# Who transposes x's second contraction tile: TensorE or the DMA, and which queue loads what first

## The chip, the cores and the metric

One core of a Trainium2 chip runs the whole kernel. The metric is the device time of one execution in microseconds. Five engines take part: TensorE (PE; its weight loads are shown as PEld), VectorE (DVE), ScalarE (ACT), GpSimd (POOL) and SyncE (SP). SP and ACT each issue DMAs on a queue of their own.

## What is computed

```python
x:  (1, 2048, 640) bf16;  w1: (640, 1728) bf16;  w2: (1728, 640) bf16
h = jnp.einsum("bsd,df->bsf", x, w1)
h = jax.nn.silu(h)
out = jnp.einsum("bsf,fd->bsd", h, w2)
```

## The kernel before

The program is a list of operations (`add(engine, emit, deps, group)`), written out by hand. Each engine executes its own operations in the order in which they were added, and before each it waits for the semaphores of its `deps`. A DMA's `group` names its semaphore. Nothing reorders the work.

TensorE needs x with the contraction on the partitions, so x is transposed into `xT_sb` in tiles of 128 contraction rows by 512 rows of x (`SCH`). There are five contraction tiles (`DT`, counted 0 to 4) and four chunks of 512 rows (`NSC`, counted from 0). Two ways of transposing are in use:

- by TensorE: x's tile is loaded as it is into `x0_sb`, four 128x128 transposes (L182) against `ident` put it into a bank of PSUM, and DVE (L186) or ACT (L188) copies it to `xT_sb`. Chunk 0 does this for tiles 0 and 1. Tile 0 is loaded in two halves, `x0_a` on SP and `x0_b` on ACT, and is copied in two halves; tile 1 is `x0_c`, on ACT.
- by DMA: `transpose_x` (L152) issues a transposing DMA on SP that reads x in HBM and writes `xT_sb`. Chunk 0 does this for tiles 2, 3 and 4 (`x0_2` to `x0_4`), the other chunks for all five.

w1 is loaded on SP: the first 6 column tiles (`FA`) of each contraction tile by itself (`w1_0` to `w1_4`, 192 KB each), the rest in `w1_a` (column tiles 6 and 7) and `w1_b` (8 to 13). On SP the order is x0_a, w1_0, w1_1, w1_2, x0_2, w1_3, x0_3, w1_4, x0_4, w1_a, w1_b, and then the transposes of chunk 1, the first of which waits for w1_a.

On TensorE come warm-up matmuls on constants (L172), the transposes of tile 0, two more warm-up matmuls, and then `column_group` (L263): for each contraction tile in turn six matmuls of 128x512, one into each of six banks. The first matmul of each contraction tile waits for x's tile and w1's tile. After the second matmul of a contraction tile, `between` is called, and there `transpose_next` puts the four transposes of the next tile, if TensorE transposes it: this is the case for tile 1 alone. `unit` (L221) does the other column tiles, five matmuls each, the first of which waits for w1_a or w1_b. ACT (sigmoid, L205) and DVE (multiplication, L208) make `hT_sb` from the banks. Chunk 1 begins with a second `column_group`, and chunks 2 and 3 use `unit` throughout. Last comes the product with w2 (L326), copied out (L337, L339) and stored (L299).

Of the kernel before, what the change touches and what calls it, by code (L numbers as in the profile page):

```python
# [20 lines left out]
class Plan:  # L21
# [9 lines left out]
    def add(self, eng, emit, deps=(), group=None):  # L31
        op = Op(eng, emit, [d for d in deps if d is not None], group)
        self.ops.append(op)
        return op
# [40 lines left out]
def bass_standalone__dense_activation_silu__prompt_kernel(  # L75
# [6 lines left out]
    bf16 = mybir.dt.bfloat16  # L82
    fp32 = mybir.dt.float32

    xf = x.flatten_outer_dims()
    of = out.flatten_outer_dims()
    S, D = xf.shape
    F = w1.shape[1]
    P = 128
    H = P // 2  # L90
    SCH = 512
    DT = D // P
# [5 lines left out]
    JB = SCH // P  # L98
# [4 lines left out]
    with ExitStack() as es:  # L103
        def sb(name, shape, dtype):
            return es.enter_context(nc.sbuf_tensor(name, shape, dtype))

        xT_sb = sb("xT_sb", [P, DT, S], bf16)
# [3 lines left out]
        NSIG = 4  # L111
        sig_sb = sb("sig_sb", [P, NSIG, SCH], bf16)
        o_sb = sb("o_sb", [P, ST, D], bf16)
        x0_sb = sb("x0_sb", [P, JB, D], bf16)
        ident = sb("ident", [P, P], bf16)
        warm_sb = sb("warm_sb", [P, 32], fp32)
        oT_sb = sb("oT_sb", [P, NSC, SCH], bf16)
        ps = es.enter_context(nc.psum_tensor("ps", [P, NBANK, SCH], fp32))

        w1_v = w1.rearrange("(dt p) f -> p dt f", p=P)  # L120
        x0_v = xf[0:SCH, :].rearrange("(j p) d -> p j d", p=P)
        w2_v = w2[0:FR * P, :].rearrange("(ft p) d -> p ft d", p=P)

        plan = Plan()
        add = plan.add
        bank_free = [[] for _ in range(NBANK)]
        turn = [0]

        def take_bank():
            b = turn[0] % NBANK  # L130
            turn[0] += 1
            return b


        FA = 6
        w1_cuts = [FA, 8, FT]
        id_a = add("pool", lambda e: e.memset(ident[:, :], 0.0))
        id_b = add("pool", lambda e: e.affine_select(
            out=ident[:, :], in_=ident[:, :], compare_op=ALU.not_equal, fill=1.0,
            base=0, pattern=[[-1, P]], channel_multiplier=1), [id_a])  # L140
        warm = add("dve", lambda e: e.memset(warm_sb[:, :], 0.0))

        def load_x0(eng, name, j0, j1, d0, d1):
            return add(eng, lambda e: e.dma_start(
                out=x0_sb[:, j0:j1, d0 * P:d1 * P], in_=x0_v[:, j0:j1, d0 * P:d1 * P]), group=name)

        def load_w1(eng, name, d0, d1, f0, f1, deps=()):
            return add(eng, lambda e: e.dma_start(
                out=w1_sb[:, d0:d1, f0:f1], in_=w1_v[:, d0:d1, f0:f1]), deps, group=name)

        def transpose_x(sc, dt, name, deps=()):
            return add("sp", lambda e: e.dma_start_transpose(  # L152
                out=xT_sb[:, dt, sc * SCH:(sc + 1) * SCH],
                in_=xf[sc * SCH:(sc + 1) * SCH, dt * P:(dt + 1) * P]), deps, group=name)

        x0_a = [load_x0("sp", "x0_a", 0, JB // 2, 0, 1), load_x0("act", "x0_b", JB // 2, JB, 0, 1)]
        w1_lo = [load_w1("sp", "w1_0", 0, 1, 0, FA * P)]
        x0_c = load_x0("act", "x0_c", 0, JB, 1, 2)
        w1_lo += [load_w1("sp", f"w1_{dt}", dt, dt + 1, 0, FA * P) for dt in (1, 2)]
        add("act", lambda e: e.activation(out=warm_sb[:, :], in_=warm_sb[:, :], func=ACT.Sigmoid), [warm])  # L160
        x0_t = {2: transpose_x(0, 2, "x0_2")}
        for dt in (3, 4):
            w1_lo.append(load_w1("sp", f"w1_{dt}", dt, dt + 1, 0, FA * P))
            x0_t[dt] = transpose_x(0, dt, f"x0_{dt}")
# [5 lines left out]
        def warm_up(columns):  # L170
            for n in columns:
                add("pe", lambda e, n=n: e.matmul(  # L172
                    ps[:, NBANK - 1, 0:n], lhsT=ones[:, 0:P], rhs=ones[:, 0:n], start=True, stop=True))

        warm_up([SCH] * 5 + [2 * P])

        def transpose_x0(dt, j0, j1, b):

            dst = ps[:, b, :].bitcast(bf16)[:, j0 * P:j1 * P]
            out = xT_sb[:, dt, j0 * P:j1 * P]  # L180
            for j in range(j0, j1):
                t = add("pe", lambda e, j=j: e.transpose(  # L182
                    dst[:, (j - j0) * P:(j - j0 + 1) * P], x0_sb[:, j, dt * P:(dt + 1) * P], ident[:, :]),
                    [x0_a[j // (JB // 2)], id_b] if dt == 0 else [x0_c] + bank_free[b])
            if dt % 2 == 0:
                c = add("dve", lambda e: e.tensor_copy(out=out, in_=dst), [t])  # L186
            else:
                c = add("act", lambda e: e.copy(out=out, in_=dst), [t])  # L188
            bank_free[b] = [c]
            return c  # L190

# [10 lines left out]
        def silu(b, parts, n, pe):  # L202
            s = sig_turn[0] % NSIG
            sig_turn[0] += 1
            a = add("act", lambda e: e.activation(  # L205
                out=sig_sb[:, s, 0:n], in_=ps[:, b, 0:n], func=ACT.Sigmoid), [pe, sig_free[s]])
            for rows, ft, cols in parts:
                v = add("dve", lambda e, rows=rows, ft=ft, cols=cols: e.tensor_tensor(  # L208
                    out=hT_sb[rows, ft, cols], in0=ps[rows, b, 0:n], in1=sig_sb[rows, s, 0:n],
                    op=ALU.mult), [a])  # L210
                chunk_done[cols.start // SCH] = v
                if ft == FR:
                    tail_done[cols.start // SCH] = v
            bank_free[b] = [v]
            sig_free[s] = v
# [25 lines left out]
        for sc in range(1, NSC):  # L241
# [4 lines left out]
            if sc == 2:  # L246
                half = FR // 2
                for a, z in ((0, half), (half, FR)):
                    w2_dma.append(add("sp", lambda e, a=a, z=z: e.dma_start(
                        out=w2_sb[:, a:z, :], in_=w2_v[:, a:z, :]), group="w2"))  # L250
                for hh in range(2):
                    w2_dma.append(add("sp", lambda e, hh=hh: e.dma_start(
                        out=w2_sb[hh * H:(hh + 1) * H, FR, :], in_=w2[FR * P:F, :]), group="w2"))

        def column_group(sc, x_dep, w1_dep, between=None):

            banks = [take_bank() for _ in range(FA)]
            for dt in range(DT):
                for ft in range(FA):
                    deps = bank_free[banks[ft]] if dt == 0 else []  # L260
                    if ft == 0:
                        deps = deps + [x_dep[dt], w1_dep[dt]]
                    pe = add("pe", lambda e, dt=dt, ft=ft: e.matmul(  # L263
                        ps[:, banks[ft], :], lhsT=w1_sb[:, dt, ft * P:(ft + 1) * P],
                        rhs=xT_sb[:, dt, sc * SCH:(sc + 1) * SCH],
                        start=(dt == 0), stop=(dt == DT - 1)), deps)
                    if dt == DT - 1:
                        silu(banks[ft], [(slice(0, P), ft, slice(sc * SCH, (sc + 1) * SCH))], SCH, pe)
                    if between and ft == 1:
                        between(dt + 1)  # L270

        def transpose_next(dt):
            if dt in x0_t:
                x0T.append(x0_t[dt])
            elif dt < DT:
                x0T.append(transpose_x0(dt, 0, JB, FA + dt % 2))

        half = [transpose_x0(0, k * JB // 2, (k + 1) * JB // 2, FA - 2 + k) for k in range(2)]
        x0T = [half[1]]
        warm_up([SCH, 2 * P])  # L280
        column_group(0, x0T, w1_lo, transpose_next)
        for ft in range(FA, FR):
            unit(0, ft, 0, SCH)

        for sc in range(1, NSC):
            if sc == 1:
                column_group(sc, x1_of, w1_lo)
            for ft in range(FA if sc == 1 else 0, FR):
                unit(sc, ft, 0, SCH)
# [112 lines left out]
```

## Time and profile before

| What | Value |
|---|---|
| median of 3 runs | 125.84 us (125.55 to 126.11) |
| the profiled execution | 126.19 us, span 124.8 us |
| TensorE busy | 121.7 us (97%), 890 matmuls |
| DVE, ACT busy | 44.7 us (36%), 38.8 us (31%) |
| DMA | 10.41 MB, mean 83 GB/s over the span |
| transposing DMAs of x (L152) | 18, issue 1.12 to 2.60 us each, landing 2.7 to 7.1 us after the start of the issue |

The profile is one execution on the chip. Times in a timeline count from the start of the span. An entry with SPq or ACTq is the issue of a DMA; when its data are there is a separate figure, the landing, counted from the start of the issue. A matmul's time holds its way through the array, so successive matmuls overlap, and the pace of TensorE is read from their starts. The profiled time is 1.4 us longer than the span; that part lies around the span.

### The profile page before, as it was taken

What the parts mean: (1) busy time and instruction counts of PE and PEld (TensorE: products, weight loads), DVE (VectorE), ACT (ScalarE), POOL (GpSimd) and SP (SyncE); (2) the same over time, 40 slices, a digit from 0 to 9 for tenths busy, and PEclk for the clock granted to TensorE, in tenths of its full rate; (3) what the DMA queues carried; (4) which work ended last, traced back from release to release, by engine and by line L of the source; (5) the groups of instructions that cost most, each with busy time, mean ns of one, the idle gap of its engine ahead of it and who ended that gap; (6) DMA issues with size and microseconds to landing.
All of it is one profiled execution on the core that took longest, in us unless ns stands there. A gap on an engine that the chain in (4) does not pass through costs nothing.

```text
span 124.8 us, 2074 instructions
## 1 busy us (share of the span) xinstructions
PE 121.7 (97%) x890; PEld 57.1 (46%) x890; DVE 44.7 (36%) x70; ACT 38.8 (31%) x68; POOL 0.7 (1%) x6
## 2 busy tenths in 40 slices
PE   7999999999999999999999999999999999999992
PEld 2444444444444444444444444444444444446481
DVE  0102984079666666666682020202021020202021
ACT  4104953097555555555530010101011010101021
POOL 2000000000000000000000000000000000000000
PEclk9999999999999999999999999999999999999999
DMA  3989682559980000000000001115120201102434
GB/s 69 293 179 347 141 102 54 114 100 373 349 170 3 0 5 0 3 0 0 0 0 5 0 2 30 26 21 181 39 105 5 105 0 21 33 15 74 158 104 112
DMA packets 20201, 10.41 MB, mean 83 GB/s; under 512 B 14432, under 2 KB 20192, under 8 KB 20192
## 3 DMA queue, kind: packets, MB, share of 16 engines
q1 hardware_dynamic: 19104, 9.95, 30.0%
q10 hardware_dynamic: 1088, 0.33, 1.1%
q8 instruction: 7, 0.11, 0.4%
q14 instruction: 2, 0.02, 0.1%
HBM read 4.77 MB, written 2.62 MB: 59 GB/s over the span
## 4 chain that ended last, share of the span: by engine, by line
PE 98%; DVE 0%; issue 0%
PE ps L326 47%; PE ps L221 35%; PE ps L263 11%; PE ps L172 3%; PE ps L231 2%; PE ps L182 1%; DVE o_sb L337 0%
## 5 line engine op out<-in xcount | busy, mean ns | idle before, releaser
L326 PE MATMUL ps<-w_sb,hT_sb 64*128 64x512 bf16 (+2 forms) x486 | 47.3, 352 | 0.0
L208 DVE TENSOR_TENSOR hT_sb<-ps,sig_sb 128x512 bf16<-128x512 f32 (+1 forms) x56 | 37.0, 688 | 25.3 <-ACT sig_sb L205 25.3
L221 PE MATMUL ps<-xT_sb,w_sb 128*128 128x512 bf16 x200 | 43.5, 379 | 0.0
L205 ACT ACTIVATE sig_sb<-ps 128x512 bf16<-128x512 f32 x54 | 30.7, 606 | 27.5 <-PE ps L221 16.4
L326 PEld LDWEIGHTS ps<-w_sb,hT_sb 64*128 64x128 bf16 x486 | 23.5, 94 | 23.5
L221 PEld LDWEIGHTS ps<-xT_sb,w_sb 128*128 128x128 bf16 x200 | 19.6, 98 | 23.6
L337 DVE CAST o_sb<-ps 128x512 bf16<-128x512 f32 (+2 forms) x9 | 5.7, 632 | 37.6 <-PE ps L326 37.6
L339 ACT CAST o_sb<-ps 128x512 bf16<-128x512 f32 (+2 forms) x9 | 4.8, 538 | 38.6 <-PE ps L326 38.6
L263 PE MATMUL ps<-xT_sb,w_sb 128*128 128x512 bf16 x60 | 14.1, 392 | 0.0
L326 PE MATMUL ps<-hT_sb,w_sb 64*128 64x512 bf16 x108 | 12.3, 376 | 0.0
L263 PEld LDWEIGHTS ps<-xT_sb,w_sb 128*128 128x128 bf16 x60 | 5.9, 101 | 7.4 <-DVE xT_sb L186 0.7
L326 PEld LDWEIGHTS ps<-hT_sb,w_sb 64*128 64x128 bf16 x108 | 5.2, 94 | 6.5 <-issue 0.4
L337 DVE CAST oT_sb<-ps 128x512 bf16<-128x512 f32 x2 | 1.4, 692 | 11.7 <-PE ps L326 11.7
L339 ACT CAST oT_sb<-ps 128x512 bf16<-128x512 f32 x2 | 1.2, 585 | 13.6 <-PE ps L326 13.6
L172 PE MATMUL ps<-const-bfloat16-1.0 128*128 128x512 bf16 (+1 forms) x8 | 3.4, 575 | 0.8 <-PEq L387 0.8
L231 PE MATMUL ps<-xT_sb,w_sb 128*64 128x512 bf16 x20 | 2.3, 381 | 0.0
L172 PEld LDWEIGHTS ps<-const-bfloat16-1.0 128*128 128x128 bf16 x8 | 1.0, 140 | 1.8 <-issue 1.8
L160 ACT ACT_TABLE_LOAD x1 | 1.3, 1283 | 1.8 <-issue 1.8
L231 PEld LDWEIGHTS ps<-xT_sb,w_sb 128*64 128x64 bf16 x20 | 1.0, 110 | 1.2 <-issue 0.4
L186 DVE COPY xT_sb<-ps 128x256 bf16<-128x256 bf16 x2 | 0.5, 292 | 2.6 <-PE ps L182 2.6
L182 PEld LDWEIGHTS ps<-ident,x_sb 128*128 128x128 bf16 x8 | 1.0, 144 | 0.9 <-DMA x_sb<-in_x_dram 0.6
L188 ACT COPY xT_sb<-ps 128x512 bf16<-128x512 bf16 x1 | 0.6, 585 | 2.5 <-PE ps L182 2.5
(9 smaller groups left out, 2.5 us busy)
## 6 DMA issues: line engine op xcount, KB each, us to landing
out_dram<-o_sb SPq DMA_DIRECT2D x14, 160.0 KB, 1.9
w_sb<-in_w_dram SPq DMA_DIRECT2D x1, 1120.0 KB, 7.7
w_sb<-in_w_dram SPq DMA_DIRECT2D x5, 192.0 KB, 3.1
w_sb<-in_w_dram SPq DMA_DIRECT2D x1, 960.0 KB, 5.6
w_sb<-in_w_dram SPq DMA_DIRECT2D x1, 880.0 KB, 5.5
w_sb<-in_w_dram SPq DMA_DIRECT2D x1, 320.0 KB, 3.7
xT_sb<-in_x_dram SPq DMA_TRANSPOSE x18, 3.0
o_sb<-oT_sb SPq DMA_TRANSPOSE x16, 2.3
```

Of the source, the lines that this page charges most:

```text
L160: add("act", lambda e: e.activation(out=warm_sb[:, :], in_=warm_sb[:, :], func=ACT.Sigmoid), [warm])
L172: add("pe", lambda e, n=n: e.matmul(ps[:, NBANK - 1, 0:n], lhsT=ones[:, 0:P], rhs=ones[:, 0:n], start=True, stop=True))
L182: t = add("pe", lambda e, j=j: e.transpose(dst[:, (j - j0) * P:(j - j0 + 1) * P], x0_sb[:, j, dt * P:(dt + 1) * P], ident[:, :]), [x0_a[j ...
L188: c = add("act", lambda e: e.copy(out=out, in_=dst), [t])
L205: a = add("act", lambda e: e.activation(out=sig_sb[:, s, 0:n], in_=ps[:, b, 0:n], func=ACT.Sigmoid), [pe, sig_free[s]])
L208: v = add("dve", lambda e, rows=rows, ft=ft, cols=cols: e.tensor_tensor(out=hT_sb[rows, ft, cols], in0=ps[rows, b, 0:n], in1=sig_sb[rows, ...
L221: pe = add("pe", lambda e, dt=dt: e.matmul(ps[:, b, 0:n], lhsT=w1_sb[:, dt, ft * P:(ft + 1) * P], rhs=xT_sb[:, dt, cols], start=(dt == 0), ...
L231: pe = add("pe", lambda e, dt=dt, hh=hh: e.matmul(ps[hh * H:(hh + 1) * H, b, :], lhsT=w1_sb[:, dt, FR * P:F], rhs=xT_sb[:, dt, (sc + hh) * ...
L263: pe = add("pe", lambda e, dt=dt, ft=ft: e.matmul(ps[:, banks[ft], :], lhsT=w1_sb[:, dt, ft * P:(ft + 1) * P], rhs=xT_sb[:, dt, sc * SCH:( ...
L326: pe = add("pe", lambda e, b=b, n=n, lhsT=lhsT, rhs=rhs, ft=ft: e.matmul(ps[:, b, 0:n], lhsT=lhsT, rhs=rhs, start=(swap == 0 and ft == 0), ...
L337: ev = add("dve", lambda e, b=b, n=n, dst=dst: e.tensor_copy(out=dst, in_=ps[:, b, 0:n]), [pe])
L339: ev = add("act", lambda e, b=b, n=n, dst=dst: e.copy(out=dst, in_=ps[:, b, 0:n]), [pe])
```

## The change

Contraction tile 1 of chunk 0 is transposed by a DMA, `x0_1`, which becomes the first on SP's queue. x's tile 0 is loaded by one DMA of 128 KB instead of two halves, first on ACT's queue, and w1's tile 0 follows it there instead of on SP. The load x0_c, the four TensorE transposes of tile 1 and ACT's copy of them go, and `column_group` has no `between` any more. One of the two warm-up matmuls behind the transposes of tile 0, that of 256 columns, goes as well. `x0_sb` keeps one tile instead of five. In the changed kernel the lines after the loads have moved up: L172 becomes L168, L182 L178, L186 L180, L221 L213 and L263 L255.

```diff
--- before.py
+++ after.py
@@ -111,14 +111,14 @@
         NSIG = 4
         sig_sb = sb("sig_sb", [P, NSIG, SCH], bf16)
         o_sb = sb("o_sb", [P, ST, D], bf16)
-        x0_sb = sb("x0_sb", [P, JB, D], bf16)
+        x0_sb = sb("x0_sb", [P, JB, P], bf16)
         ident = sb("ident", [P, P], bf16)
         warm_sb = sb("warm_sb", [P, 32], fp32)
         oT_sb = sb("oT_sb", [P, NSC, SCH], bf16)
         ps = es.enter_context(nc.psum_tensor("ps", [P, NBANK, SCH], fp32))
 
         w1_v = w1.rearrange("(dt p) f -> p dt f", p=P)
-        x0_v = xf[0:SCH, :].rearrange("(j p) d -> p j d", p=P)
+        x0_v = xf[0:SCH, 0:P].rearrange("(j p) d -> p j d", p=P)
         w2_v = w2[0:FR * P, :].rearrange("(ft p) d -> p ft d", p=P)
 
         plan = Plan()
@@ -140,10 +140,6 @@
             base=0, pattern=[[-1, P]], channel_multiplier=1), [id_a])
         warm = add("dve", lambda e: e.memset(warm_sb[:, :], 0.0))
 
-        def load_x0(eng, name, j0, j1, d0, d1):
-            return add(eng, lambda e: e.dma_start(
-                out=x0_sb[:, j0:j1, d0 * P:d1 * P], in_=x0_v[:, j0:j1, d0 * P:d1 * P]), group=name)
-
         def load_w1(eng, name, d0, d1, f0, f1, deps=()):
             return add(eng, lambda e: e.dma_start(
                 out=w1_sb[:, d0:d1, f0:f1], in_=w1_v[:, d0:d1, f0:f1]), deps, group=name)
@@ -153,12 +149,12 @@
                 out=xT_sb[:, dt, sc * SCH:(sc + 1) * SCH],
                 in_=xf[sc * SCH:(sc + 1) * SCH, dt * P:(dt + 1) * P]), deps, group=name)
 
-        x0_a = [load_x0("sp", "x0_a", 0, JB // 2, 0, 1), load_x0("act", "x0_b", JB // 2, JB, 0, 1)]
-        w1_lo = [load_w1("sp", "w1_0", 0, 1, 0, FA * P)]
-        x0_c = load_x0("act", "x0_c", 0, JB, 1, 2)
+        x0_t = {1: transpose_x(0, 1, "x0_1")}
+        x0_a = add("act", lambda e: e.dma_start(out=x0_sb[:, :, :], in_=x0_v), group="x0_a")
+        w1_lo = [load_w1("act", "w1_0", 0, 1, 0, FA * P)]
         w1_lo += [load_w1("sp", f"w1_{dt}", dt, dt + 1, 0, FA * P) for dt in (1, 2)]
         add("act", lambda e: e.activation(out=warm_sb[:, :], in_=warm_sb[:, :], func=ACT.Sigmoid), [warm])
-        x0_t = {2: transpose_x(0, 2, "x0_2")}
+        x0_t[2] = transpose_x(0, 2, "x0_2")
         for dt in (3, 4):
             w1_lo.append(load_w1("sp", f"w1_{dt}", dt, dt + 1, 0, FA * P))
             x0_t[dt] = transpose_x(0, dt, f"x0_{dt}")
@@ -174,18 +170,14 @@
 
         warm_up([SCH] * 5 + [2 * P])
 
-        def transpose_x0(dt, j0, j1, b):
+        def transpose_x0(j0, j1, b):
 
             dst = ps[:, b, :].bitcast(bf16)[:, j0 * P:j1 * P]
-            out = xT_sb[:, dt, j0 * P:j1 * P]
+            out = xT_sb[:, 0, j0 * P:j1 * P]
             for j in range(j0, j1):
                 t = add("pe", lambda e, j=j: e.transpose(
-                    dst[:, (j - j0) * P:(j - j0 + 1) * P], x0_sb[:, j, dt * P:(dt + 1) * P], ident[:, :]),
-                    [x0_a[j // (JB // 2)], id_b] if dt == 0 else [x0_c] + bank_free[b])
-            if dt % 2 == 0:
-                c = add("dve", lambda e: e.tensor_copy(out=out, in_=dst), [t])
-            else:
-                c = add("act", lambda e: e.copy(out=out, in_=dst), [t])
+                    dst[:, (j - j0) * P:(j - j0 + 1) * P], x0_sb[:, j, :], ident[:, :]), [x0_a, id_b])
+            c = add("dve", lambda e: e.tensor_copy(out=out, in_=dst), [t])
             bank_free[b] = [c]
             return c
 
@@ -252,7 +244,7 @@
                     w2_dma.append(add("sp", lambda e, hh=hh: e.dma_start(
                         out=w2_sb[hh * H:(hh + 1) * H, FR, :], in_=w2[FR * P:F, :]), group="w2"))
 
-        def column_group(sc, x_dep, w1_dep, between=None):
+        def column_group(sc, x_dep, w1_dep):
 
             banks = [take_bank() for _ in range(FA)]
             for dt in range(DT):
@@ -266,19 +258,11 @@
                         start=(dt == 0), stop=(dt == DT - 1)), deps)
                     if dt == DT - 1:
                         silu(banks[ft], [(slice(0, P), ft, slice(sc * SCH, (sc + 1) * SCH))], SCH, pe)
-                    if between and ft == 1:
-                        between(dt + 1)
-
-        def transpose_next(dt):
-            if dt in x0_t:
-                x0T.append(x0_t[dt])
-            elif dt < DT:
-                x0T.append(transpose_x0(dt, 0, JB, FA + dt % 2))
-
-        half = [transpose_x0(0, k * JB // 2, (k + 1) * JB // 2, FA - 2 + k) for k in range(2)]
-        x0T = [half[1]]
-        warm_up([SCH, 2 * P])
-        column_group(0, x0T, w1_lo, transpose_next)
+
+        half = [transpose_x0(k * JB // 2, (k + 1) * JB // 2, FA - 2 + k) for k in range(2)]
+        x0T = [half[1]] + [x0_t[dt] for dt in range(1, DT)]
+        warm_up([SCH])
+        column_group(0, x0T, w1_lo)
         for ft in range(FA, FR):
             unit(0, ft, 0, SCH)
```

## The prediction

> **What bounds the kernel now.** I read the page's busy time and chain first, then the chain in order of time, then the timeline of the first 14 us and the landing of each DMA issued there. TensorE is busy 121.7 of 124.8 us and the chain is TensorE's all the way, so only two things can move the end: fewer cycles on TensorE, or a wait in front of it.
>
> From the page and the chain in order of time (start, us, what):
>
> ```profile
> PE 98%; DVE 0%; issue 0%
> PE ps L326 47%; PE ps L221 35%; PE ps L263 11%; PE ps L172 3%; PE ps L231 2%; PE ps L182 1%; DVE o_sb L337 0%
> ...
> 4.35 1.01 PE ps L263 x2
> 5.36 0.43 PE ps L182 x4
> 5.79 6.27 PE ps L263 x28
> 12.06 7.55 PE ps L221 x35
> 19.61 6.47 PE ps L263 x30
> ```
>
> The change ends before 12.06: from there the matmuls are the same in number and order. The first group of 30 (L263) takes 7.7 us from 4.35, the second, the same 30 matmuls, 6.47. The difference is the four transposes (L182, 0.43) and a slow start. The timeline (start, us, engine, line) shows the rest:
>
> ```profile
> 0.73 0.46 SPq L144 DMA_DIRECT2D x_sb<-in_x_dram  x1
> 0.74 1.03 ACTq L144 DMA_DIRECT2D x_sb<-in_x_dram  x2
> 0.77 2.51 PE L172 MATMUL ps<-const-bfloat16-1.0 128*128 128x512 bf16 x6 [0.77 <-PEq L387]
> 1.26 1.40 SPq L148 DMA_DIRECT2D w_sb<-in_w_dram  x3
> 2.70 1.21 SPq L152 DMA_TRANSPOSE xT_sb<-in_x_dram  x1
> 2.92 0.52 PEld L182 LDWEIGHTS ps<-ident,x_sb 128*128 128x128 bf16 x4 [0.33 <-DMA x_sb<-in_x_dram]
> 3.53 0.51 DVE L186 COPY xT_sb<-ps 128x256 bf16<-128x256 bf16 x2 [2.63 <-PE ps L182]
> ...
> 4.32 0.14 PEld L263 LDWEIGHTS ps<-xT_sb,w_sb 128*128 128x128 bf16 x2 [0.67 <-DVE xT_sb L186]
> 4.35 1.01 PE L263 MATMUL ps<-xT_sb,w_sb 128*128 128x512 bf16 x2
> ...
> 7.52 1.15 SPq L148 DMA_DIRECT2D w_sb<-in_w_dram  x2
> ```
>
> The six warm-up matmuls start 0.42 us apart. In narrow windows the L263 matmuls start at 4.35, 4.73, 5.58, 6.01, 6.28, and from 6.28 on eight take 1.89, 0.216 apart. So TensorE runs at half its later pace until about 6.1, 5.3 us after its first matmul, while the granted clock in the rows reads 1.00 throughout. DVE is done at 4.04, so the wait put down to it at 4.32 is really w1_0 (issue to landing, us):
>
> ```profile
> w_sb<-in_w_dram SPq DMA_DIRECT2D x1, 192.0 KB, 3.0
> x_sb<-in_x_dram ACTq DMA_DIRECT2D x1, 128.0 KB, 3.3
> xT_sb<-in_x_dram SPq DMA_TRANSPOSE x1, 3.7
> w_sb<-in_w_dram SPq DMA_DIRECT2D x1, 320.0 KB, 3.7
> w_sb<-in_w_dram SPq DMA_DIRECT2D x1, 880.0 KB, 5.5
> ```
>
> These are w1_0 (issued 1.26, landed 4.2), x0_c (1.27), the transpose x0_2 (2.70), and w1_a and w1_b. w1_a is issued at 7.52 and lands at 11.2, 0.7 before its matmul at 11.90. w1_b is issued at 8.15 and lands at 13.6; its matmul comes ten later, at 14.06, and that one's weights load one matmul ahead, at 13.84. So w1_b has about 0.2 us to spare, the least of the lead-in.
>
> **Part by part.**
>
> *Four TensorE transposes and the 256-column warm-up go.* The transposes take 0.43 us at half pace, between the second and third matmul. Matmuls move into that place and leave from the fast stretch: 0.43 of slow time is one matmul, worth 0.216 later. Gain 0.21 us. The warm-up (0.21) filled the wait for w1_0; without work ready it becomes idle time and costs nothing. ACT's copy L188 (0.58) goes too, off the path: its tile was ready at 6.41, for a matmul at 6.72.
>
> *x's tile 0 whole on ScalarE's queue.* Same 128 KB as the two halves, which landed after 2.1 and 2.3 us, but x0_1 moves another 128 KB beside it on the other queue. Below: 2.3 (landed 3.04). Above: 3.7, the transpose beside weight loads (4.4). In the stretch from 2.86 to 4.35 the DMA moved 296 GB/s, so 128 KB more is 0.44 us; I take 2.8, landing at 3.55, nearest to the half loads because nothing stands ahead of it on its queue. All four transposes now wait for all of it. The warm-up matmuls run out at 3.07: an idle hole of 0.5 us. From the first transpose to the last copy's end took 0.96 (3.07 to 4.04), so tile 0 is ready at 4.5; the warm-up matmul that is left covers most of that.
>
> *w1's tile 0 on ScalarE's queue.* Second there, issued again at 1.27 since the first issue takes 0.5. Ahead of it on its queue stand 128 KB instead of 64; on the other queue x0_1 replaces half of tile 0 and x0_c. Below: 2.95, as now (4.2). Above: 0.44 for a whole tile more (4.65). I take 4.6, since x0_1 now comes ahead of it where x0_c came beside it. First matmul 4.65 instead of 4.35.
>
> The sum for the group: starts 4.65, 5.08, 5.50, 5.93, fast from 6.2. Four matmuls are out by 6.2; before, four were out by 6.28. So 0.3 us of delay at half pace costs 0.15, the missing transposes return 0.21: the group ends 0.06 to 0.08 earlier.
>
> *x0_1 first on SyncE's queue.* A transpose takes 1.12 to 1.26 us to issue (2.70 to 3.95 with the gap behind it); it replaces x0_a and w1_0, which held SP from 0.73 to 1.75. Everything behind moves 0.2 later: w1_1, w1_2, x0_2, w1_3, x0_3, w1_4, x0_4, w1_a, w1_b and the x1 transposes. x0_1 itself lands 3.0 to 3.7 after issue, by 4.4; it is needed at 4.65 + 6 x 0.43 less the faster pace, about 6.5. w1_1 (5.1, then 5.3), x0_2 (6.4, then 6.6, for about 7.8) and w1_3 to x0_4 (9.3, then 9.5, for 10.5) all land over a microsecond early or nearly so. w1_a at 11.45 still leads its weight load at 11.6. **w1_b is what is late next**: 13.8 against a weight load wanted at 13.77. It takes back 0 to 0.1. x1_0 goes from 14.57 to 14.8, needed at 19.4. Nothing else moves past a queue; POOL and DVE keep their work.
>
> Total: 0.07 gained, 0.05 given back: no change, with ends of -0.35 (all lands as early as now, w1_b hidden) and +0.3. The profiled execution is 126.19 us with a span of 124.8; 1.4 lie around it. The three runs have a median of 125.84, 0.35 below it. On the median: 125.8.
>
> **Rivals.**
>
> *Early data (0.14).* Both loads land as now; the first matmul starts at 4.1. For it: the bytes up to w1_0 are nearly the same. Gain 0.21 + 0.12, of which w1_b, due then at 13.5, takes back up to 0.3: 125.5.
>
> *Late data (0.12).* x0_a and w1_0 are held up by the transpose on the other queue, by up to a microsecond (3.7 instead of 2.8). For it: x0_2, issued right behind w1_2, is the slowest 128 KB of the lead-in. The hold costs half while TensorE is slow: 0.5 - 0.2 = 0.3; 126.2. The Trainium skill ("DMA: Bandwidth & Descriptors", Queues, rings and completion order) says that an engine's completion increment lands only after all its earlier writes, on whichever queue. By that rule x0_a's signal would wait for pieces of x0_1 in front of it; no trace here has a transpose issued beside a load from the other queue, so it stays untested.
>
> *The fast pace comes later (0.20), slower.* TensorE was never idle for more than 0.2 us (4.14 to 4.35) in the 5.3 us before its pace doubled. The changed kernel leaves a hole at 3.07 of about 0.5 and perhaps one at 4.4. If the pace needs work without a hole of that size, counting starts anew at 3.55 or at 4.65: the pace doubles 2.8 to 3.9 us later, and half of that is lost, 1.4 to 1.9. Time 127.2 to 127.7. It decides once x0_a lands well after 3.3. Against it: the 0.2 hole did no harm. The Trainium skill ("TensorE: Matmul & The Clock Gate", Part 1) has the clock released after a busy window of about 3.4 us that runs free of the kernel; by that rule a spoilt window costs half of 3.4, an estimate of 1.7 us and 127.5, and the moment varies from run to run.
>
> *SP's first transpose issues slowly (0.05), slower.* L152's issues range from 1.12 to 2.60 us. At 2.60 all of SP moves 1.6 later, w1_b lands at 15.2 and TensorE, fast by then, stands 1.3: 127.1. The slow one lay at 17.6, in a busy stretch, so it is unlikely here.
>
> *The pace doubles sooner (0.07), faster.* If TensorE transposes delay the faster pace, then with four fewer it could come with the first matmuls, at 4.65 instead of 6.1: half of 1.45 is 0.7; 125.1. Nothing in the trace speaks for it but that eight transposes lie in the slow stretch. That x0_1 isn't really first can be left out: its issue has nothing ahead of it on SP.
>
> **How the numbers follow.** About 0.5% (0.6 us) is what a measurement of this kernel can tell from no change. The forecast has 0.42, the rivals above the rest. Faster: 0.07, a share of 0.06 from early data and 0.02 of the forecast, 0.15. Slower: 0.20 + 0.05, 0.04 from late data and 0.03 of the forecast, 0.32. Same: 0.53. Range 125.2 to 127.2: it takes in all of the forecast, early and late data, the slow issue and the near end of the late pace; it leaves out its far end (0.1) and the sooner pace (0.07).
>
> **What would show it.** In the new profile: the tile-0 transposes at about 3.5, the first L255 matmul near 4.65 with thirty in an unbroken row, the 0.216 spacing from about 6.1, w1_b landing near 13.8 with a wait under 0.1. Fast spacing only after 9 would be the late pace; a first matmul after 5.2, late data; a first SP issue over 2 us, the slow transpose. I am wrong in the sum if the second column group starts more than 0.3 away from 19.45.

## The result, and the profile after

| | kernel before | changed kernel |
|---|---|---|
| median | 125.84 us (125.47 to 126.56, 21 runs) | 126.39 us (125.97 to 127.59, 21 runs) |
| profiled execution, span | 126.19, 124.8 | 126.39, 125.1 |

The ratio is 1.0047, with an interval of 1.0029 to 1.0066: slower by 0.37 to 0.83 us. The forecast was no change, 125.8. The time lies between 125.2 and 127.2, but the slowdown was not forecast. Here and below, an execution more than 1.5% above its kernel's fastest is left out of the ratio.

The chain of the changed kernel, from the page and then in order of time (start, us, what), where the kernel before had TensorE alone:

```profile
PE 94%; DMA 3%; ACTq 0%; DVE 0%; issue 0%
...
1.24 3.16 DMA w_sb<-in_w_dram
4.40 0.14 issue
4.53 7.44 PE ps L255 x30
11.97 2.25 PE ps L213 x10
14.22 0.01 issue
14.23 5.56 PE ps L213 x25
19.79 6.47 PE ps L255 x30
```

The DMA in it is the load of w1_0, for which the first matmul waited in the kernel before as well. Ten matmuls behind the first group take 2.25 instead of the 2.16 that 0.216 each makes, because they begin 0.08 late; the eleventh, the first with columns of w1_b, starts at 14.23 and not at 14.05, ten times 0.216 behind the first. The second column group is in the chain at 19.79 instead of 19.61, so 0.18 is lost by then. The timeline shows both places (start, us, engine, line; idle before and what ended it in brackets):

```profile
0.73 1.21 SPq L148 DMA_TRANSPOSE xT_sb<-in_x_dram  x1
0.74 0.47 ACTq L153 DMA_DIRECT2D x_sb<-in_x_dram  x1
1.24 0.53 ACTq L144 DMA_DIRECT2D w_sb<-in_w_dram  x1
2.00 1.03 SPq L144 DMA_DIRECT2D w_sb<-in_w_dram  x2
3.26 0.34 PEld L178 LDWEIGHTS ps<-ident,x_sb 128*128 128x128 bf16 x4 [0.68 <-DMA x_sb<-in_x_dram]
...
4.53 7.44 PE L255 MATMUL ps<-xT_sb,w_sb 128*128 128x512 bf16 x30 [0.24 <-DMA w_sb<-in_w_dram]
...
7.84 1.15 SPq L144 DMA_DIRECT2D w_sb<-in_w_dram  x2
...
11.88 1.84 PEld L213 LDWEIGHTS ps<-xT_sb,w_sb 128*128 128x128 bf16 x10 [0.41 <-DMA w_sb<-in_w_dram]
...
14.20 5.09 PEld L213 LDWEIGHTS ps<-xT_sb,w_sb 128*128 128x128 bf16 x25 [0.48 <-DVE hT_sb L200]
```

The group itself does what the sum said: an unbroken row of thirty, whose last matmul gives way at 11.81 (before: 11.90). Then the weight load for w1_a's columns waits until 11.88, and the one for w1_b's until 14.20. The profile puts the second wait down to DVE, but this matmul needs the first bank of the group again, and DVE began the multiplication that frees it at 11.56 and takes 0.69 for one. What came just before 14.20 is w1_b, landed at 14.10. The landings (us from issue) of x0_a, w1_0, w1_a and w1_b:

```profile
x_sb<-in_x_dram ACTq DMA_DIRECT2D x1, 128.0 KB, 2.5
w_sb<-in_w_dram ACTq DMA_DIRECT2D x1, 192.0 KB, 3.2
w_sb<-in_w_dram SPq DMA_DIRECT2D x1, 320.0 KB, 4.0
w_sb<-in_w_dram SPq DMA_DIRECT2D x1, 880.0 KB, 5.6
```

w1_a lands at 11.84 (before: 11.24) and w1_b at 14.10 (13.61). Both were issued only 0.31 later.

This single pair accounts for 0.18 of 0.55 us. The profiled execution of the kernel before was itself 0.35 above its median, and that turned out to matter.

### The profile page after: what moved, and what is told of

It is laid out like the page before. It is cut to its first block, busy times and chain, and to the rows that moved or that the text cites. A ratio compares the mean times of both kernels' runs of the same rounds, so it can differ in the third digit from the quotient of the medians.

```text
span 125.1 us, 2062 instructions
## 1 busy us (share of the span) xinstructions
PE 121.6 (97%) x885; PEld 56.1 (45%) x885; DVE 44.8 (36%) x70; ACT 38.3 (31%) x67; POOL 0.7 (1%) x6
## 3 DMA queue, kind: packets, MB, share of 16 engines
HBM read 4.64 MB, written 2.62 MB: 58 GB/s over the span
## 4 chain that ended last, share of the span: by engine, by line
PE 94%; DMA 3%; ACTq 0%; DVE 0%; issue 0%
PE ps L310 47%; PE ps L213 35%; PE ps L255 11%; DMA w_sb<-in_w_dram 3%; PE ps L223 2%; ACTq L153 0%; DVE o_sb L321 0%
## 5 line engine op out<-in xcount | busy, mean ns | idle before, releaser
L213 PE MATMUL ps<-xT_sb,w_sb 128*128 128x512 bf16 x200 | 43.7, 379 | 0.0
L213 PEld LDWEIGHTS ps<-xT_sb,w_sb 128*128 128x128 bf16 x200 | 19.4, 98 | 24.0 <-DVE hT_sb L200 0.5
L255 PE MATMUL ps<-xT_sb,w_sb 128*128 128x512 bf16 x60 | 14.1, 394 | 0.2 <-DMA w_sb<-in_w_dram 0.2
L255 PEld LDWEIGHTS ps<-xT_sb,w_sb 128*128 128x128 bf16 x60 | 6.0, 101 | 8.3 <-issue 1.1
L168 PE MATMUL ps<-const-bfloat16-1.0 128*128 128x512 bf16 (+1 forms) x7 | 3.1, 594 | 0.8 <-PEq L371 0.8
L168 PEld LDWEIGHTS ps<-const-bfloat16-1.0 128*128 128x128 bf16 x7 | 0.9, 136 | 1.9 <-issue 1.9
L180 DVE COPY xT_sb<-ps 128x256 bf16<-128x256 bf16 x2 | 0.5, 292 | 2.8 <-PE ps L178 2.8
L178 PEld LDWEIGHTS ps<-ident,x_sb 128*128 128x128 bf16 x4 | 0.3, 130 | 0.7 <-DMA x_sb<-in_x_dram 0.7
L178 PE MATMUL ps<-ident,x_sb 128*128 128x128 bf16 x4 | 0.6, 307 | 0.0
```

Of the source, the lines that this page charges most:

```text
L168: add("pe", lambda e, n=n: e.matmul(ps[:, NBANK - 1, 0:n], lhsT=ones[:, 0:P], rhs=ones[:, 0:n], start=True, stop=True))
L178: t = add("pe", lambda e, j=j: e.transpose(dst[:, (j - j0) * P:(j - j0 + 1) * P], x0_sb[:, j, :], ident[:, :]), [x0_a, id_b])
L213: pe = add("pe", lambda e, dt=dt: e.matmul(ps[:, b, 0:n], lhsT=w1_sb[:, dt, ft * P:(ft + 1) * P], rhs=xT_sb[:, dt, cols], start=(dt == 0), ...
L255: pe = add("pe", lambda e, dt=dt, ft=ft: e.matmul(ps[:, banks[ft], :], lhsT=w1_sb[:, dt, ft * P:(ft + 1) * P], rhs=xT_sb[:, dt, sc * SCH:( ...
```

## The experiments

Two theories were to be told apart. **A**: what SyncE issues behind x0_1 lands later than TensorE wants it. **C**: the idle holes that the change leaves on TensorE ahead of the first group delay its faster pace. A third, **B**, put the loss on the later first matmul (4.53 instead of 4.35). An execution is called early or late here by the moment at which TensorE's pace doubles, from one matmul of 512 columns in 0.43 us to one in 0.216. Each kernel was timed beside the kernel before on the same chip.

**w1's tile 1 on ScalarE's queue** takes A's cause out of the changed kernel.

```diff
-w1_lo += [load_w1("sp", f"w1_{dt}", dt, dt + 1, 0, FA * P) for dt in (1, 2)]
+w1_lo += [load_w1("act", "w1_1", 1, 2, 0, FA * P), load_w1("sp", "w1_2", 2, 3, 0, FA * P)]
```

> The changed kernel with w1's tile 1 issued third on ScalarE's queue instead of second on SyncE's, so that everything behind it on SyncE's queue is issued about 0.6 us earlier. Theory A (w1_a and w1_b, issued 0.3 us later than before, land after TensorE wants them): w1_b is issued near 7.85, lands near 13.4, TensorE's two waits at 11.8 and 14.1 go, and the time falls from 126.4 to about 125.9. Theory B (the first L255 matmul comes later, 4.53 instead of 4.35): the first matmul still starts at 4.5 and the time stays at 126.4. Theory C (the idle hole ahead of the tile-0 transposes delays the faster pace): hole and time unchanged, 126.4.

Median 125.97 beside 125.92, ratio 1.0022 (0.9994 to 1.0051). w1_a is issued at 7.40 and w1_b at 8.02, 0.44 earlier; they land at 11.17 and 13.52, about 0.6 earlier, and both waits are gone from the chain:

```profile
4.40 7.52 PE ps L255 x30
11.93 7.55 PE ps L213 x35
19.48 6.47 PE ps L255 x30
```

A's prediction holds. The first matmul came at 4.40, so B is not yet ruled out. Three of 12 executions took 127.0 to 128.0; these long ones are C's question.

**w1_b cut in two** is meant to shorten only the last wait. (The names of the loads, and the index by which chunk 1's transposes go on waiting for w1_a, change with it.)

```diff
-w1_cuts = [FA, 8, FT]
+w1_cuts = [FA, 8, 10, FT]
```

> The changed kernel with w1_b cut in two, column tiles 8 and 9 (320 KB) and the rest; the x1 transposes wait for w1_a as they did. Theory A: the first piece lands near 12.7, the wait at 14.1 goes, that for w1_a at 11.8 stays; 0.2 to 0.4 us less, 126.0 to 126.2. Theories B and C: 126.4, as neither the first matmul nor the pace is touched.

125.88 beside 125.92, ratio 1.0004 (0.9988 to 1.0020): the whole loss is gone, with both holes left, where A expected 0.2 to 0.4. Why so much isn't shown; in the trace w1_a lands at 11.55, 0.3 before the earliest of the other traces with the same issue time, and whether the smaller load behind it has a part in that was not tested. The trace is of an early execution. TensorE's pace doubles before the first real matmul at 4.23, not at 6.1, and thirty matmuls at 0.216 would be done at 10.7. It then runs into the loads (weight loads, idle before and what ended it):

```profile
9.82 0.98 PEld L255 LDWEIGHTS ps<-xT_sb,w_sb 128*128 128x128 bf16 x6 [0.74 <-DMA xT_sb<-in_x_dram]
11.59 1.41 PEld L213 LDWEIGHTS ps<-xT_sb,w_sb 128*128 128x128 bf16 x8 [0.79 <-DMA w_sb<-in_w_dram]
```

The last contraction tile of x landed at 9.78. So the moment at which the pace doubles differs between executions, and where it comes early, the loads set the end of the lead-in alone.

**Later issue alone, in the kernel before** (two small DMAs ahead of w1_a).

```diff
+for k in range(2):
+    add("sp", lambda e, k=k: e.dma_start(
+        out=pad_sb[:, k * 16:(k + 1) * 16], in_=xf[0:P, k * 16:(k + 1) * 16]), group=f"pad{k}")
 w1_dma = [load_w1("sp", f"w1_{name}", ...
```

> The kernel before, with two DMAs of 4 KB into an unused tile ahead of w1_a on SyncE's queue, so that w1_a and w1_b are issued about 1.1 us later and nothing else changes before them. Theory A: w1_a lands near 12.3 and w1_b near 14.7, TensorE waits about 0.8 us in all, 126.5 to 126.7. Theories B and C: first matmul and pace as before, 125.8.

126.54 beside 125.92, ratio 1.0059 (1.0043 to 1.0075). The time is as A had it, though w1_a landed at 11.94 and w1_b at 14.35, earlier than expected: 1.1 us of later issue became 0.7 of later landing. In this trace the first matmul came at 4.14, earlier than in the kernel before, and no hole was added, so B and C have nothing to offer for the loss.

**The first hole filled, in the changed kernel** (`warm_up([SCH] * 6)` for `warm_up([SCH] * 5 + [2 * P])`).

> The changed kernel with the last of the six warm-up matmuls at 512 columns instead of 256, so that TensorE is busy until 3.29 and the hole before the tile-0 transposes (3.07 to 3.27) is gone. Theory C: the faster pace comes earlier or more evenly, and the time falls toward 125.9. Theories A and B: the transposes start at most 0.05 later, the waits for w1_a and w1_b stay, 126.4.

126.19, ratio 1.0026 (1.0010 to 1.0042), against 1.0047 of the changed kernel, timed at another time: between the theories, with overlapping intervals. The waits for w1_a (landed 11.88) and w1_b (14.16) are there in the trace, as A says.

**A warm start, tried first with 24 matmuls ahead.** All loads wait for 16 copies on ScalarE, while TensorE runs on constants. (Shortened: the first loads on each queue get `[go]` as a dependency as well.)

```diff
+for k in range(16):
+    go = add("act", lambda e, k=k: e.copy(out=scr2_sb[:, k, :], in_=scr_sb[:, :]), [scr])
+for k in range(24):
+    add("pe", lambda e: e.matmul(...constants...))
-warm_up([SCH] * 5 + [2 * P])
+warm_up([SCH] * 11, [go])
```

> The kernel before, started warm: 24 constant matmuls on TensorE and 16 copies on ScalarE come first, and all loads and the warm-up matmuls (11 of 512 columns now) wait for the last copy, so that the faster pace has begun before the first load and the moment at which it begins no longer matters. This is the base for the next kernel: about 10 us over the kernel before. All theories: TensorE runs at 0.216 from its first real matmul, and waits for w1_a or w1_b some 0.3 us or less.

> The changed kernel with the same warm start. Theory A (x0_1 at the head of SyncE's queue makes w1_4, x0_4, w1_a and w1_b land 0.4 to 0.6 later, and TensorE stands for that in full when it is fast early): 0.4 to 0.6 us slower than the warm kernel before. Theory C (the idle hole delays the faster pace): no difference, since the pace is fast in both. The prediction's own sum (0.2 us later issue, nearly all of it hidden): within 0.2 us of the warm kernel before.

135.52 and 135.97, 0.45 apart; the ratios to the kernel before without a warm start, 1.0764 (1.0730 to 1.0798) and 1.0779 (1.0750 to 1.0808), do not tell them apart. The control was not clean: in the second kernel's trace TensorE stood idle from 7.7 to 10.5 and then ran slowly again. The columns are the stretch, its length, busy time (and count) of TensorE, the granted clock, the DMA share and GB/s:

```profile
7.50:10.40 2.90, 0.19 (x1) 1.00 0.00 0
10.75:14.10 3.35, 3.35 (x9) 0.50 0.75 181
14.15:16.00 1.85, 1.59 (x11) 1.00 0.98 244
```

**The warm start again, with 32 matmuls ahead and 8 behind**, for the kernel before, the changed kernel, and the changed kernel with w1_1 on ScalarE's queue.

> The kernel before, started warm again, now with 32 constant matmuls ahead and 8 warm-up matmuls of 512 columns behind the wait, so that TensorE is idle less than 1.5 us before the loads start and stays at its fast pace. Base for the next two, about 135.5 us. All theories: no spacing of 0.427 after the loads start; waits of TensorE for w1_a or w1_b remain.

> The changed kernel started warm in the same way. Theory A (w1_a and w1_b land 0.4 to 0.6 later than in the kernel before, and TensorE at its fast pace stands for them in full): 0.4 to 0.6 us over the warm kernel before, the second column group 0.4 to 0.6 later counted from the first load's issue, with waits that end on w1_a and w1_b in both. Theory C (idle holes and pace): no difference. The prediction's sum: within 0.2 us.

> The changed kernel with w1's tile 1 third on ScalarE's queue, started warm. Theory A: w1_a and w1_b land as in the warm kernel before, the 0.4 to 0.6 us go, time equal to the warm kernel before within 0.15 us. If the delay came from the added transpose itself or from the later first matmul rather than from what stands behind x0_1 on SyncE's queue: it stays at 0.4 to 0.6 over it.

Medians 135.35, 135.95 and 135.81; ratios to the kernel before without a warm start 1.0744 (1.0718 to 1.0771), 1.0797 (1.0760 to 1.0835) and 1.0756 (1.0731 to 1.0780). With the pace fast from the first real matmul, the changed kernel is still 0.6 slower by the medians, which C alone does not give; the intervals of the two ratios just overlap. By the ratios w1_1 on ScalarE's queue takes back three quarters, by the medians only 0.14; with five and six executions each, that is as far as this goes. The three traces came out nearly alike (the second column group at 29.33, 29.25 and 29.23) and do not show the 0.4 to 0.6 that A expected. That of the kernel before was one of its two longest executions of six (135.9), with w1_a landing at 21.53 instead of the 21.03 in the first warm trace, at the same issue time; there the second group came at 28.88. A single landing moves by half a microsecond by itself.

**Both holes filled, with w1_1 on ScalarE's queue.**

> The changed kernel with w1's tile 1 on ScalarE's queue, as in the first experiment, and the two holes of the lead-in filled: six warm-up matmuls of 512 columns, and 512 and 256 columns behind the transposes of tile 0. Theory C for the long executions alone (127 and more, 3 of 12 with w1_1 on ScalarE, 2 of 21 of the changed kernel, none of 29 before): they go, and the median falls below 125.9. Theory A alone: the median stays at 125.9 to 126.0, and the long executions stay as often.

126.00 beside 126.06, ratio 0.9995 (0.9977 to 1.0012), longest 126.49. The long executions went; the ratio is lower than in the first experiment, with the holes (1.0022), but the intervals overlap.

**Two candidates.** The first also puts w1's tile 2 on ScalarE's queue and cuts w1_b; the second is the kernel above with the cut alone.

> A candidate to beat both: the changed kernel with w1's tiles 1 and 2 on ScalarE's queue, w1_b cut at column tile 10, and both holes filled. Theory A: w1_a is issued near 6.8 and lands near 10.7, no wait is left behind the first group, the median falls to 125.3 to 125.6. Theories B and C without A: about 125.9.

> A candidate to beat both: w1's tile 1 on ScalarE's queue, both holes filled, and w1_b cut at column tile 10. Theory A: the wait for w1_b goes as well, 125.6 to 125.8, against 125.9 to 126.0 for the kernel before. Theory C alone: 126.0, as with the holes filled alone.

126.42 (1.0033, 1.0009 to 1.0056) and 125.99 (1.0006, 0.9985 to 1.0027). Neither beats the kernel before. In the first, w1_a lands at 10.69 as expected, but x0_2 took 5.8 us to land instead of 3.4, at 7.84: weights from ScalarE's queue share the DMA engines with it. An execution whose pace doubles early wants x0_2 at 4.46 + 12 x 0.216 = 7.05 and would wait 0.8; the trace is of a late one (6.4), so this wait is worked out, not seen. The Trainium skill ("DMA: Bandwidth & Descriptors", Issuing engines are not separate DMA queues) says that DMAs of several engines interleave on the same DMA engines and that a second issuing engine saves only the time to issue; the 5.8 agrees.

**Holes alone, later issue alone, and the changed kernel with and without holes**, together on one chip.

```diff
 # holes in the kernel before
-warm_up([SCH] * 5 + [2 * P])
+warm_up([SCH] * 4)
-warm_up([SCH, 2 * P])
+warm_up([SCH])
 # later issue in the kernel before
+add("sp", lambda e: e.dma_start(out=pad_sb[:, :], in_=xf[0:P, 0:16]), group="pad")
 x0_t = {2: transpose_x(0, 2, "x0_2")}
 # holes filled in the changed kernel
-warm_up([SCH] * 5 + [2 * P])
+warm_up([SCH] * 6)
-warm_up([SCH])
+warm_up([SCH, 2 * P])
```

> The kernel before with holes and nothing else: four warm-up matmuls of 512 columns instead of five and one of 256, and one of 512 behind the transposes of tile 0 instead of 512 and 256, so that TensorE is idle from about 2.5 to 3.07 and from 3.93 to 4.35. All loads are issued and land as before. Theory C (idle time ahead of the first group delays the faster pace in a share of the executions): slower by 0.2 to 0.5 us, with single executions over 127. Theory A alone: no change, 125.9 to 126.0.

> The changed kernel as it is, as the base beside the next one on the same chip and for one more trace. All theories: 126.3 to 126.5; w1_a lands near 11.6 to 11.9, w1_b near 14.0 to 14.2.

> The changed kernel with both holes filled: six warm-up matmuls of 512 columns, and 512 and 256 columns behind the transposes of tile 0. Loads as in the changed kernel. Theory A alone: equal to the changed kernel beside it within 0.1 us. Theories A and C together: 0.2 to 0.3 us below it, 126.1 to 126.2, and no execution over 127; what is left over the kernel before, about 0.3, is the later landing of w1_a and w1_b.

> The kernel before with one DMA of 4 KB into an unused tile on SyncE's queue ahead of x0_2, so that x0_2, w1_3, x0_3, w1_4, x0_4, w1_a and w1_b are issued about 0.47 us later, some 0.15 more than in the changed kernel. The holes stay as small as before. Theory A: w1_a and w1_b land 0.3 to 0.5 later, 0.3 to 0.5 us slower, 126.3 to 126.4. Theory C alone: no change.

| kernel | median | ratio to the kernel before (126.10) |
|---|---|---|
| before, holes alone | 126.44 | 1.0023 (1.0005 to 1.0041) |
| changed, again | 126.72 | 1.0045 (1.0024 to 1.0067) |
| changed, holes filled | 126.59 | 1.0039 (1.0018 to 1.0059) |
| before, later issue alone | 126.53 | 1.0034 (1.0023 to 1.0045) |

The last three came out 0.1 to 0.4 us above the times expected for them, but so did the kernel before beside them (126.10, on other chips 125.84 to 126.06). The later issue alone costs 0.43 us in the kernel before, with a delay of 0.5 against the change's 0.31 and the warm-up matmuls as they were. In its trace the pace doubles at 3.7, and TensorE waits for w1_a at 11.97 and for w1_b at 14.49:

```profile
11.97 2.33 PE L223 MATMUL ps<-xT_sb,w_sb 128*128 128x512 bf16 x10 [0.36 <-DMA w_sb<-in_w_dram]
14.49 0.81 PE L223 MATMUL ps<-xT_sb,w_sb 128*128 128x512 bf16 x3 [0.19 <-DMA w_sb<-in_w_dram]
```

The second trace of the changed kernel is an execution whose pace doubles earlier, at 5.4, and it is no faster for it. It waits for w1_a until 12.14, and its second group starts at 19.87, 0.42 later than in the trace of the kernel before:

```profile
4.48 7.07 PE L255 MATMUL ps<-xT_sb,w_sb 128*128 128x512 bf16 x30 [0.15 <-DMA w_sb<-in_w_dram]
...
12.14 3.14 PE L213 MATMUL ps<-xT_sb,w_sb 128*128 128x512 bf16 x13 [0.59 <-DMA w_sb<-in_w_dram]
```

Its chain begins with the issue of x0_1 and runs over SyncE's issues, one after the other, to the landing of w1_a and, in this count, to the second group at 20.03, against 19.61 before:

```profile
0.73 1.22 SPq L148
...
7.86 4.24 DMA w_sb<-in_w_dram
...
12.14 2.33 PE ps L213 x10
...
20.03 6.47 PE ps L255 x30
```

This is A's path, seen in one execution.

Holes alone cost something too, 0.3 by the medians, and in that trace the pace doubles only at 6.9; these holes are larger than the changed kernel's first (0.56 and 0.42 against 0.2 and 0.4). Filling the holes of the changed kernel took 0.13 off here, inside its interval and less than the 0.2 to 0.3 expected with C.

Whether holes make single executions long stays open. Executions of 127.2 to 127.6 us were 4 of 33 of the changed kernel and 1 of 12 with w1_1 on ScalarE's queue, against 1 of 55 of the five kernels with one or both holes filled and none of 120 of the kernel before. That speaks for C. Against it, none of 12 was longer than 127.0 with w1_b cut and both holes left, nor with the larger holes in the kernel before, where C expected single ones over 127. The four longest executions of all fell on kernels with and without holes alike: 129.78 of the changed kernel and 127.98 with w1_1 on ScalarE's queue, 128.59 of the kernel before and 128.14 of it with the later issue. No long execution was traced.

**What the landings say together**, for the kernels that load w1_b whole, without a warm start or a small DMA ahead of it:

| order on SyncE's queue | issue of w1_a, w1_b | landing of w1_a | landing of w1_b |
|---|---|---|---|
| before (2 traces) | 7.53, 8.15 | 11.24, 11.43 | 13.61, 14.04 |
| changed (4 traces) | 7.84, 8.47 | 11.84, 11.88, 12.03, 12.10 | 14.10, 14.16, 14.33, 14.34 |
| changed, w1_1 on ScalarE (2 traces) | 7.40, 8.02 | 11.17, 11.56 | 13.52, 13.85 |

On the means the change moves w1_a by 0.6 and w1_b by 0.4, from few traces: with w1_b cut, w1_a landed at 11.55 in the changed kernel, and in the two warm traces of the changed kernel it landed 3.8 us after its issue, no later than in the kernel before. The two kernels before with later issue alone landed w1_a at 11.92 and 11.94 and w1_b at 14.36 and 14.35, close to the changed kernel, and they lose as much as it, 0.43 and 0.62, though their issue was 0.5 and 1.1 late: the time goes with the landing.

Where TensorE's pace doubles early it should stand for this in full, since the first group then waits for loads anyway and the saved transposes return nothing: 0.42 in the trace above. Where it doubles late, 0.18 is left. This is worked out; no early execution of the kernel before as it is was traced. A mixture of 0.18 and 0.4 to 0.6 covers much of the 0.55, and a share from the holes could cover the rest. That A's part is the larger is shown from both sides: the loss goes when w1_1 moves to ScalarE's queue or w1_b is cut, with both holes left (1.0022 and 1.0004), and it comes in the kernel before with the later issue alone. The warm pairs point the same way, weakly. C's share of the median is not settled.

## Why the prediction went wrong, by its steps

*Right.* The group's working: tile 0 landed at 3.22 (forecast 3.55), w1_0 at 4.40 (4.6), the first matmul came at 4.53 (4.65) and the group ended 0.09 earlier (0.06 to 0.08). w1_b was named as what is late next. SP's first transpose took 1.21 to issue, so the slow-issue rival is out. Early data and late data were not what happened: the first matmul came near 4.5, where early data had 4.1, and x0_a landed 1.3 before x0_1 (4.49), which was issued at the same time on the other queue, so it was not held for the transpose as a whole. The pace doubled at 6.2 in the profiled execution, not sooner than before; early executions exist in kernels with all eight TensorE transposes too (3.7 with the later issue alone).

*The term that was mis-sized* is what the later issue on SyncE's queue takes back: "It takes back 0 to 0.1", for w1_b, with w1_a put down as just in time. Issue moved by 0.31, not 0.2: the transpose held SP to 1.94, and w1_1 and w1_2 behind it started at 2.00 and 2.62, 0.62 apart where they were 0.47 apart before. And the landing moved by more than the issue, 0.6 and 0.5 in the profiled pair, while the sum moved landings by the issue alone; why it did is not shown. In the profiled execution this cost 0.08 + 0.18 instead of 0 to 0.1, which less the 0.09 gained leaves the 0.18 lost. The sign named for an error in the sum, a second column group more than 0.3 from 19.45, did not show: it started at 19.62. The rest of the loss lies outside that pair.

*The assumption under it* was that the slack read from the trace, 0.2 us at w1_b and 0.4 at w1_a, belongs to the kernel. It belongs to one execution, whose pace doubled at 6.1 and whose time was 0.35 over the median. That difference was noted in the sum and only subtracted. As the matmuls behind the lead-in are the same, an execution 0.35 shorter most likely has a shorter lead-in, hence less slack or none. Among the traces the doubling came anywhere between 3.7 and 6.9. With it early, the gain of 0.21 for the transposes is gone as well.

*The late pace* was a rival at 0.20, priced at 1.4 to 1.9 as if it struck every execution. The holes came out at 0.2 us (3.07 to 3.27) and 0.4 (4.1 to 4.53), the first below the point given for it, and the profiled pace doubled at 6.2, as before. What the runs show is weaker: 0.3 for larger holes put into the kernel before, and perhaps a tail. The rule of the Trainium skill drawn on there ("TensorE: Matmul & The Clock Gate", Part 1), a busy window of about 3.4 us that runs free of the kernel, agrees with the traces in part: the first matmul starts at 0.77 or 0.78 in all of them, the pace doubles at unequal moments, and the slow stretch in the first warm try lasts 3.4 us. But the earliest doubling, at 3.7, comes 2.9 us after the first matmul, sooner than a whole busy window allows.

## What to carry to other kernels

Slack that one trace shows in front of an in-order engine holds for that execution; if the engine's start-up varies, ask what the slack is when it is fastest, and count the stall there. A transpose put at the head of a DMA queue pays with its issue time for everything behind it, and here the payer was not the next load but the last of the lead-in, 13 us later. Moving loads to another queue gave the issue time back here but not the bandwidth: with two of w1's tiles on ScalarE's queue, x0_2 took 5.8 us to land instead of 3.4.

## What was not expected of the hardware

TensorE's pace doubles at a moment that differs between the traces by 3 us (3.7 to 6.9, with the first matmul at 0.77 or 0.78), while the first slow stretch reads a granted clock of 1.00. After 2.8 us without a matmul (7.7 to 10.5, first warm try), the clock was granted at 0.50 for about 3.4 us (10.7 to 14.1) under a full load of matmuls, and that stretch does read 0.50. A load's landing moved by 0.5 us between executions at an equal issue time (w1_a 21.03 and 21.53 in the two warm kernels before).
